# Parking weight sums whole, copying the second weights a batch later, and making the sums of u on VectorE

## The chip, the cores and the metric

The kernel runs on one core of a Trainium2 chip. The metric is the device time of one execution in microseconds. Three runs of the kernel before took 598.86, 599.93 and 600.01; the median is 599.93.

## The reference

A local attention feeds a mixer of two pairs of linear layers. All tensors are float32.

```python
# q, k, v: (4, 8, 768, 64); block, window = 32, 16
k_sum = k.reshape(B, H, nb, block, D).max(axis=3)
v_sum = v.reshape(B, H, nb, block, D).mean(axis=3)
mask_l = np.abs(pos[:, None] - pos[None, :]) < window
scores = concat([where(mask_l, scale * q @ k.T, -1e9), scale * q @ k_sum.T + log(block)])
x = softmax(scores) @ concat([v, v_sum])              # -> x: (4, 768, 512)
# mixer, w_tok1 (768, 256), w_tok2 (256, 768), w_ch1 (512, 1536), w_ch2 (1536, 512)
h = np.maximum(x.transpose(0, 2, 1) @ w_tok1, 0.0) @ w_tok2
u = x + h.transpose(0, 2, 1)
out = u + np.maximum(u @ w_ch1, 0.0) @ w_ch2
```

## The kernel before

**A planner orders the work.** Each piece of work is handed to `add(engine, took, run, reads, writes, rank, behind, kb)`. `Plan._order` then walks a model of the five queues (`pe`, `act`, `dve`, `pool`, `sp`): a work becomes ready when what it reads has been written and its tile is free, each queue takes the ready work of the lowest rank, then the earliest added, and the result is a fixed order per engine. `took` is the model's duration. A DMA costs `sp` 0.06 us of the model, and all DMAs share one line: `dma = max(dma, now) + w.kb / self.RATE` with `RATE` 250 (KB per us), and `LAND` 2.2 us on top. The ranks are `R_H, R_EVAC, R_ATT, R_LATER, R_W, R_BACK`, from 0 to 5; DMAs have rank 0. `behind` orders without waiting for the end: `state["gate"]` holds back parts of a slot's side work until that slot's first matmul has been started in the model. Tiles have tags with a number of buffers ("h" 2, "t1" 4, "u0" 4, "e" 3, "w1" and "w2" 12); the n-th tile of a tag waits until all users of the tile that many places before it are done.

**Precision.** A float32 operand is split into a high part rounded to `float32r` (an ACT copy) and a low part (the difference). Each product is then three matmuls (`HL`): high by high, high by low, low by high.

**Stages.** The four batches run one after the other, `b` = 0 to 3. In a batch of the first three the mixer's second pair of layers has 24 slots: `half` 0 (512 columns) with `f` = 0 to 11, then `half` 1 (256 columns). A slot is `ch1` (twelve matmuls to bank `hp`, line 852, then `h` split on ACT, line 864, and DVE, line 869) and `ch2` (twelve matmuls into `acc`, line 895). Beside the slots of batch `b` runs all that batch `b + 1` needs before its own: attention (`att_step`: `scores`, `turn_blocks`, `weighted`), `tok1x` and `tok2`, which give `u`. From the third batch on (`FAR`), the probabilities `e` are turned through DRAM: a DVE block transpose (line 511), one DMA to `away`, four fetches to `eT` (line 530), and then the `av` products (line 557); `x` goes the same way by `xaway` to `xT`, or to the tiles `u` (`u32`) of the last batch. `finish` adds `acc` to `u` on DVE (line 926, tile `ot` of tag "h"), adds the low part on POOL (line 934) and stores (line 945).

**The last batch** multiplies in 2 x 2 blocks with seven products instead of eight (`last_mix`). It needs sums of weight blocks (`s1` to `s4`) for both layers, and sums of `u` blocks (`t_1` to `t_4`, each split). Every product of six matmuls is ordered after the one before it. In the first phase each of six `k` has the products "11", "s2", "s3", "12", "s1" and, one `k` later by `later(k)`, "s4" and "22". Their banks are `pa`, `pb`, `pc`. `from_bank` (line 1098, DVE) adds a bank to a tile. In the second phase each of the seven names has six `k`, with banks `qa`, `qb`, `qc`; its right side is split just before use into tiles `x..` of tag "u0" (lines 1083 and 975).

**The weight sums** are made ahead by `weight_sums(w, k, tag)`, twelve calls at the slots `SUMS = ((14, 17), (6, 8, 10, 13, 15), (6, 8, 10, 12, 14))` of the three batches: five POOL and six DVE operations on 128x256 (`between`, lines 973 and 975), two ACT roundings (line 1035), two POOL differences (line 1040), and four DMAs of 256 KB to `sums` (line 1048). `weight_away(f)` copies the split second weights, 512 KB each, to `w2d` (line 1057) in slots 0 to 11 of the second batch. `first_load` fetches both parts of `s1` to `s4` for the first phase (line 1170, tags "t1" and "u1"), `second_loads` fetches the second phase's weights (line 1209, `rs` from `sums` and `r` from `w2d`) into the tiles that held the first weights.

Of the kernel before, what the change touches and what calls it, by code (L numbers as in the profile page):

```python
# [23 lines left out]
P = 128  # L24
# [165 lines left out]
def tile_attention_mixer(  # L190
# [788 lines left out]
    def weight_sums(w, k, tag):  # L979

        blk, keys = blocks(w, k)
        away = sd[w, k] = plan.slot(dram, [P, 2, 4, 256], F32, "sums", f"sums_{w}_{k}", 2 * HALF)
        gate = state["gate"]
        one = {}

        def part(name, i):
            return (lambda: blk[name](i)), keys

        def pair(n):
            if tag == "t1":  # L990
                lo, hi = (
                    sbuf([P, 2, 256], tag, f"s{x}_{w}_{k}_{n}", 4) for x in "lh"
                )
                views = [lambda: lo.t, lambda: hi.t]
                slots = (lo, "lo"), (hi, "hi")
            else:
                slot = sbuf([P, 2, 2, 256], tag, f"s_{w}_{k}_{n}", 2)
                views = [lambda: slot.t[:, 0], lambda: slot.t[:, 1]]
                slots = (slot, "lo"), (slot, "hi")
            return views, [[(s, (x, i)) for i in range(2)] for s, x in slots]  # L1000

        for n in range(2):
            (lo, hi), (lkeys, hkeys) = pair(n)
            one[n] = lo, hi, lkeys, hkeys

            def own(i, lo=lo, lkeys=lkeys):
                return (lambda: lo()[:, i]), [lkeys[i]]

            def old(i, x):
                lo0, hi0, lk0, hk0 = one[0]  # L1010
                return ((lambda: lo0()[:, i]), [lk0[i]]) if x else ((lambda: hi0()[:, i]), [hk0[i]])

            def step(eng, i, left, right, op, lo=lo, lkeys=lkeys):
                add(
                    eng, 0.78 if eng == "pool" else 0.36,
                    lambda: between(eng, lo()[:, i], left[0](), right[0](), op),
                    reads=left[1] + right[1], writes=[lkeys[i]], rank=R_BACK, behind=gate,
                )

            if n == 0:  # L1020
                step("pool", 0, part("21", 0), part("22", 0), ALU.add)
                step("pool", 0, own(0), part("21", 1), ALU.add)
                step("pool", 0, own(0), part("22", 1), ALU.add)
                step("pool", 1, own(0), part("11", 0), ALU.subtract)
                step("pool", 1, own(1), part("11", 1), ALU.subtract)
            else:
                step("dve", 0, part("11", 0), part("21", 0), ALU.subtract)
                step("dve", 0, own(0), part("11", 1), ALU.add)
                step("dve", 0, own(0), part("21", 1), ALU.subtract)
                step("dve", 1, part("12", 0), old(1, 0), ALU.subtract)  # L1030
                step("dve", 1, own(1), old(1, 1), ALU.subtract)
                step("dve", 1, own(1), part("12", 1), ALU.add)
            add(
                "act", 0.65,
                lambda lo=lo, hi=hi: nc.scalar.activation(hi().bitcast(F32R), lo(), AF.Copy),  # L1035
                reads=lkeys, writes=hkeys, rank=R_BACK,
            )
            add(
                "pool", 1.3,
                lambda lo=lo, hi=hi: nc.gpsimd.tensor_tensor(  # L1040
                    out=lo().bitcast(F32R), in0=lo(), in1=hi(), op=ALU.subtract
                ),
                reads=hkeys, writes=lkeys, rank=R_BACK,
            )
            for i, (view, vkeys) in enumerate(((hi, hkeys), (lo, lkeys))):
                add(
                    "sp", 0.06,
                    lambda i=i, n=n, view=view: nc.sync.dma_start(
                        out=away.t[:, i, 2 * n : 2 * n + 2], in_=view()
                    ),  # L1050
                    reads=vkeys, writes=[(away, (n, i))], kb=262,
                )
# [8 lines left out]

    def last_mix():

        b = B - 1
        order = []

        def pe(took, run, reads, writes):
            order.append(
                add("pe", took, run, reads=reads, writes=writes, rank=R_W, behind=order[-1:])
            )  # L1070

        def both(eng, out_, left, right, op, rank):
            (o, oi), (l, li), (r, ri) = out_, left, right
            add(
                eng, 1.05 if eng == "pool" else 0.5,
                lambda: between(eng, o.t[:, oi], l.t[:, li], r.t[:, ri], op),
                reads=[left, right], writes=[out_], rank=rank,
            )

        def split(src, view, keys, eng, rank=R_EVAC):  # L1080
            s, i = src
            add(
                "act", 0.44, lambda: nc.scalar.activation(view(0), s.t[:, i], AF.Copy),
                reads=[src], writes=keys[:1], rank=rank,
            )
            add(
                eng, 1.05 if eng == "pool" else 0.5,
                lambda: between(
                    eng, view(1), s.t[:, i], view(0).bitcast(F32), ALU.subtract
                ),  # L1090
                reads=[src, keys[0]], writes=keys[1:], rank=rank,
            )
# [28 lines left out]
        def piece(slot, pre=()):  # L1121
            def view(i):
                t = slot.t
                for k in pre:
                    t = t[:, k]
                return t[:, i]

            return view, [(slot, (*pre, i)) if pre else (slot, i) for i in range(2)]

        B11, B12, B21, B22 = u32[0, 0], u32[1, 0], u32[0, 1], u32[1, 1]  # L1130
        tmp = sbuf([P, 4, HS], "wt", "t32", 3)
        tmp3 = sbuf([P, 2, HS], "h", "t33", 2)
        x2s = sbuf([P, 2, 2, HS], "x", "t_2", 2, F32R)
        x3s = sbuf([P, 2, 2, HS], "x", "t_3", 2, F32R)
        ops = {
            "11": [piece(u_t.pop((b, 0, j))) for j in range(2)],
            "21": [piece(u_t.pop((b, 0, 2 + j))) for j in range(2)],
            "22": [piece(u_t.pop((b, 1, 2 + j))) for j in range(2)],
            "t2": [piece(x2s, (j,)) for j in range(2)],
            "t3": [piece(x3s, (j,)) for j in range(2)],  # L1140
        }
        for j in range(2):
            both("dve", (tmp, j), (B12, j), (B11, j), ALU.subtract, R_ATT)
            both("dve", (tmp, 2 + j), (B22, j), (tmp, j), ALU.subtract, R_ATT)
            split((tmp, 2 + j), *ops["t2"][j], "dve", R_ATT)
        for j in range(2):
            both("pool", (tmp3, j), (B22, j), (B12, j), ALU.subtract, R_ATT)
            split((tmp3, j), *ops["t3"][j], "pool", R_ATT)
        ops["t1"] = [piece(sbuf([P, 2, HS], "e", f"t_1_{j}", 3, F32R)) for j in range(2)]
        ops["t4"] = [  # L1150
            piece(sbuf([P, 2, HS], *(("e", "t_4_0", 3), ("h", "t_4_1", 2))[j], F32R))
            for j in range(2)
        ]
        for j in range(2):
            split((tmp, j), *ops["t1"][j], "dve", R_ATT)
            both("dve", (tmp3, j), (B21, j), (tmp, 2 + j), ALU.subtract, R_ATT)
            split((tmp3, j), *ops["t4"][j], "pool", R_ATT)


        RING = ("s2", "s4", "s3", "s1")  # L1160

        def first_load(k):
            tag = ("t1", "u1")[k % 2]
            away, got = sd[1, k], {}
            for name in RING:
                slot = got[name] = sbuf([P, 2, 2, P], tag, f"{name}_{k}", 4, F32R)
                i = int(name[1]) - 1
                add(
                    "sp", 0.06,
                    lambda slot=slot, i=i: nc.sync.dma_start(  # L1170
                        out=slot.t.bitcast(F32).rearrange("p i c f -> p i (c f)"),
                        in_=away.t[:, :, i],
                    ),
                    reads=[(away, (i // 2, j)) for j in range(2)], writes=[(slot, 0)], kb=262,
                )
            return got
# [16 lines left out]
        def second_loads():  # L1193
            for name, _, _ in SECOND:
                for m in range(HALF // 2):
                    slot = wring[name, m] = sbuf([P, 2, 2, 256], "w1", f"r{name}_{m}", NF, F32R)
                    for j in range(2):
                        k = 2 * m + j
                        if name[0] == "s":
                            away, i = sd[2, k], int(name[1]) - 1  # L1200
                            src, keys = (lambda away=away, i=i: away.t[:, :, i]), [(away, (i // 2, x)) for x in range(2)]
                        else:
# [3 lines left out]
                            keys = [(away, 0)]  # L1206
                        add(
                            "sp", 0.06,
                            lambda slot=slot, j=j, src=src: nc.sync.dma_start(
# [318 lines left out]
    for b in range(B - 1):  # L1528
# [19 lines left out]
        for slot, (half, f) in enumerate(seq):  # L1548
# [54 lines left out]
            if b == 1 and slot < NF:  # L1603
                weight_away(slot)
# [64 lines left out]
```

## Time and profile before

| | |
|---|---|
| profiled execution | 600.4 us |
| its span | 598.6 us |
| mean granted TensorE clock | 0.977 |
| TensorE matmuls busy | 567.8 us, 95% |
| VectorE (DVE) busy | 371.2 us, 62% |
| GpSimd (POOL) busy | 260.8 us, 44% |
| ScalarE (ACT) busy | 257.0 us, 43% |
| DMA | 112.12 MB, 187 GB/s on average |
| `sums` written | 48 DMAs of 256 KB |
| `sums` read | 48 DMAs of 256 KB |
| `w2d` written | 12 DMAs of 512 KB |

The span runs from the first to the last instruction; the execution's time has 1.8 us more around it. All times in the views count from the span's start. The first batch's slots end at about 207 us, the second's at about 332, the third's at about 498; from there the last batch's two phases run, the second from 550. A row of the timeline gives start, duration, engine, line, operation, tile written from tiles read, and in brackets how long the engine had stood idle before it and what ended that.

### The profile page before, as it was taken

The page shows a single profiled execution, that of the slowest core. Times are in us where ns is not written, and L with a number is a line of the kernel's source. Part 1 is how long each engine was busy: PE and PEld are TensorE (multiplying, and loading weights), DVE is VectorE, ACT ScalarE, POOL GpSimd, SP SyncE. Part 2 cuts the span into 40 slices and gives each one's busy share as a digit, 9 for nine tenths or more (in the row PEclk, how much of TensorE's full clock was granted, in tenths as well). Part 3 has the DMA queues.
Part 4 walks back from the last instruction along what each step waited for, and adds up shares of the span by engine and source line. Part 5 has one row for each costly group of instructions (what it writes and reads, how often), then busy time and mean ns, then how long its engine had stood idle before and what let it go on. Part 6 is the DMA issues. An engine that isn't in the chain of part 4 may idle for free.

```text
span 598.6 us, 12794 instructions
## 1 busy us (share of the span) xinstructions
PE 567.8 (95%) x4629; PEld 495.2 (83%) x4629; DVE 371.2 (62%) x1006; ACT 257.0 (43%) x777; POOL 260.8 (44%) x301
## 2 busy tenths in 40 slices
PE   8899999989999999999999769999999997999997
PEld 4688878768889978877999647777789986999997
DVE  4688799986874353586354445457564862335875
ACT  4667575445674242333244224343343332334542
POOL 0225586745365210344646700034449834344611
PEclk8889999999999999999999988999999998999999
DMA  8943568644755157888839754677675533578731
GB/s 268 324 148 121 181 199 261 220 146 160 244 177 193 60 187 224 225 294 262 258 100 277 168 113 134 140 182 203 190 190 147 140 124 124 187 230 270 245 105 73
DMA packets 143375, 112.12 MB, mean 187 GB/s; under 512 B 88656, under 2 KB 118992, under 8 KB 143312
## 3 DMA queue, kind: packets, MB, share of 16 engines
q1 hardware_dynamic: 143168, 111.10, 62.3%
q8 instruction: 37, 0.61, 0.4%
q14 instruction: 26, 0.21, 0.1%
q10 hardware_dynamic: 144, 0.20, 0.1%
HBM read 74.90 MB, written 34.60 MB: 183 GB/s over the span
## 4 chain that ended last, share of the span: by engine, by line
PE 64%; DVE 11%; DMA 8%; POOL 6%; issue 3%; SPq 3%; ACT 3%; DVEq 0%; POOLq 0%; ACTq 0%
PE acc L895 17%; PE hp L852 17%; PE sc L426 3%; PE av L557 3%; PE pb L1115 3%; PE qb L1115 3%; DMA w<-in_w_ch 3%; PE qa L1115 2%; PE t1q L747 2%; PE pc L1115 2%; PE pa L1115 2%; PE qc L1115 2%; PE up L791 2%; POOL ot L934 2%; DVE wb L1451 1%
## 5 line engine op out<-in xcount | busy, mean ns | idle before, releaser
L852 PE MATMUL hp<-u,w 128*128 128x512 f32 (+1 forms) x864 | 166.7, 342 | 2.8 <-DVE u L975 1.5
L895 PE MATMUL acc<-h,w 128*128 128x512 f32 (+1 forms) x864 | 165.9, 341 | 3.2 <-DVE h L869 2.2
L852 PEld LDWEIGHTS hp<-u,w 128*128 128x128 f32 x864 | 134.4, 190 | 25.0 <-DVE u L975 2.6
L895 PEld LDWEIGHTS acc<-h,w 128*128 128x128 f32 x864 | 133.4, 189 | 24.8 <-DVE h L869 3.2
L450 ACT ACTIVATE e<-e,den 128x120 f32<-128x120 f32 x192 | 73.3, 384 | 48.1 <-DVE den L440 48.0
L869 DVE SCALAR_TENSOR_TENSOR h<-hp,h 128x512 fp32r<-128x512 f32 (+1 forms) x72 | 39.7, 551 | 68.0 <-ACT h L864 67.7
L864 ACT ACTIVATE h<-hp 128x512 fp32r<-128x512 f32 (+1 forms) x72 | 35.0, 487 | 94.6 <-PE hp L852 94.6
L440 DVE CUSTOM_DVE_ANT_0 e<-sc,mask_sb 128x120 f32<-128x120 f32 x192 | 41.5, 276 | 9.5 <-PE sc L426 5.5
L1480 POOL TENSOR_TENSOR w<-wb,w 128x256 fp32r<-128x256 f32 x48 | 37.9, 810 | 17.8 <-ACT w L1474 17.5
L791 PE MATMUL up<-wt,t 128*128 128x512 f32 (+2 forms) x192 | 40.4, 353 | 1.9 <-DVE t L686 1.4
L934 POOL TENSOR_TENSOR ot<-ot,u 128x512 f32<-128x512 f32 (+1 forms) x24 | 23.8, 1020 | 29.0 <-DVE ot L926 29.0
L450 ACT ACTIVATION_READ_ACCUMULATOR e<-e,den 128x1 f32 x192 | 36.2, 188 | 0.0
L791 PEld LDWEIGHTS up<-wt,t 128*128 128x128 f32 x192 | 31.1, 192 | 5.4 <-DVE t L686 1.9
L1040 POOL TENSOR_TENSOR sl<-sl,sh 128x512 fp32r<-128x512 f32 x12 | 15.5, 1289 | 44.0 <-ACT sh L1035 44.0
L747 PE MATMUL t1q<-xs,ws 128*128 128x256 f32 x216 | 29.4, 285 | 4.0 <-POOL ws L733 3.4
L747 PEld LDWEIGHTS t1q<-xs,ws 128*128 128x128 f32 x216 | 27.2, 190 | 5.4 <-POOL ws L733 4.2
L557 PEld LDWEIGHTS av<-v,eT 120*64 120x64 f32 x768 | 24.0, 138 | 8.0 <-issue 5.6
L557 PE MATMUL av<-v,eT 120*64 120x64 f32 x768 | 26.6, 224 | 4.2 <-DMA eT<-away 2.2
L426 PE MATMUL sc<-k,q 64*64 64x120 f32 x768 | 28.4, 275 | 1.8 <-PE et L488 0.7
L426 PEld LDWEIGHTS sc<-k,q 64*64 64x64 f32 x768 | 20.9, 135 | 10.4 <-issue 5.9
L570 DVE TENSOR_TENSOR x<-av,rec 128x384 f32<-128x384 f32 x32 | 17.4, 552 | 18.7 <-PE av L557 17.6
L1474 ACT ACTIVATE w<-wb 128x256 fp32r<-128x256 f32 x48 | 18.1, 413 | 23.8 <-DVE wb L1451 23.7
(141 smaller groups left out, 919.6 us busy)
## 6 DMA issues: line engine op xcount, KB each, us to landing
w<-in_w_ch SPq DMA_DIRECT2D x48, 256.0 KB
k<-in_kw SPq DMA_DIRECT2D x16, 720.0 KB
v<-in_vw SPq DMA_DIRECT2D x32, 288.0 KB
q<-in_q SPq DMA_DIRECT2D x16, 384.0 KB
sums<-s SPq DMA_DIRECT2D x24, 256.0 KB
w2d<-w SPq DMA_DIRECT2D x12, 512.0 KB
away<-e SPq DMA_DIRECT2D x16, 384.0 KB
eT<-away SPq DMA_DIRECT2D x64, 96.0 KB
```

Of the source, the lines that this page charges most:

```text
L426: nc.tensor.matmul(tiles[j].t[c * QT : (c + 1) * QT, i * NC : (i + 1) * NC], lhsT=qt.t[rows, t * QT : (t + 1) * QT], rhs=kt.t[rows, t, :], ...
L440: nc.vector.tensor_tensor_reduce(out=e.t[:, j, i * P : i * P + NC], in0=tiles[j].t[:, i * NC : (i + 1) * NC], in1=mask_sb[:, mv, :], op0=A ...
L450: nc.scalar.activation(ei, ei, AF.Exp, bias=den_t[n].t[:, 1, T : T + 1], scale=-1.0, accum_out=den_t[n].t[:, 0, T : T + 1],)
L557: nc.tensor.matmul(pv[cs, T], lhsT=eT[:NC, T % (TT // 2), cs], rhs=v.t[:NC, 2 * T + c], start=True, stop=True,)
L747: nc.tensor.matmul(pt.t[:, 2 * P * k : 2 * P * (k + 1)], lhsT=ws[:, wp, T, ks], rhs=xs[:, xp, T], start=(c == 0 and k == 0 and T == 0 and ...
L791: nc.tensor.matmul(pt.t[:, :nt], lhsT=t1.t[:, part, ks], rhs=wt2[w].t[:, k, h0 : h0 + nt], start=(far and k == 0 and i == 0), stop=(k == D ...
L852: nc.tensor.matmul(pt.t[:, :nt], lhsT=w1_t[f].t[:, w, c], rhs=us[c].t[:, part], start=(i == 0), stop=(i == len(ops) - 1),)
L869: lambda: nc.vector.scalar_tensor_tensor(out=h.t[:, 1], in0=pt.t[:, :nt], scalar=0.0, in1=h.t[:, 0].bitcast(F32), op0=ALU.max, op1=ALU.sub ...
L895: nc.tensor.matmul(slot.t[:, c0 : c0 + nt], lhsT=w2_t[f].t[:, w, o * P : (o + 1) * P], rhs=h.t[:, part], start=(f == 0 and w == 0 and part ...
L934: lambda view=view, u=u: nc.gpsimd.tensor_tensor(out=view(), in0=view(), in1=u.t[:, 1].bitcast(F32), op=ALU.add),
L1115: nc.tensor.matmul(bank_.t[:, :HS], lhsT=w(i), rhs=x(j), start=first and n == 0, stop=True, skip_group_check=True,)
L1480: lambda hi=hi, lo=lo, source=source: nc.gpsimd.tensor_tensor(out=lo(), in0=source(), in1=hi().bitcast(F32), op=ALU.subtract),
```

## The change

Five things are changed.

1. `weight_sums` parks each sum as whole float32. The ACT rounding and POOL difference are gone, each pair of sums is one DMA of 256 KB instead of two, and `s4` is made from the whole `s2` in two DVE operations instead of three. In the slots with tag "h" one tile holds all four sums where there were two tiles; with tag "t1" two tiles instead of four.
2. `parted` splits a parked sum after it has been fetched: in the first phase an ACT copy and a DVE difference on 256 columns for each of 24 fetches (rank `R_EVAC`), in the second phase on 512 columns for each of 12 tiles (rank `R_LATER`). The fetches of sums are 128 KB each instead of 256.
3. `weight_away` is called in slots 12 to 23 of the third batch instead of slots 0 to 11 of the second.
4. The sums of `u` move from the start of `last_mix` to `last_sums`, called in slot 22 of the third batch, ahead of that batch's `finish`. The difference for `t_3` and the low parts of `t_3` and `t_4`, six operations, go from POOL to DVE. The helpers `both`, `split` and `piece` are moved out of `last_mix` unchanged.
5. The second phase's product "11" for `k` 0 and 1 is ordered ahead of `later(5)`, the end of the first phase.

```diff
     def weight_sums(w, k, tag):
...
-        away = sd[w, k] = plan.slot(dram, [P, 2, 4, 256], F32, "sums", f"sums_{w}_{k}", 2 * HALF)
+        away = sd[w, k] = plan.slot(dram, [P, 4, 256], F32, "sums", f"sums_{w}_{k}", 2 * HALF)
...
+        if tag == "t1":
+            z = [sbuf([P, 2, 256], tag, f"s_{w}_{k}_{n}", 4) for n in range(2)]
+            at = [(z[i // 2], i % 2) for i in range(4)]
+        else:
+            z = sbuf([P, 4, 256], tag, f"s_{w}_{k}", 2)
+            at = [(z, i) for i in range(4)]
...
+        step("pool", 0, part("21", 0), part("22", 0), ALU.add)
+        step("pool", 0, own(0), part("21", 1), ALU.add)
+        step("pool", 0, own(0), part("22", 1), ALU.add)
+        step("dve", 2, part("11", 0), part("21", 0), ALU.subtract)
+        step("dve", 2, own(2), part("11", 1), ALU.add)
+        step("dve", 2, own(2), part("21", 1), ALU.subtract)
+        step("pool", 1, own(0), part("11", 0), ALU.subtract)
+        step("pool", 1, own(1), part("11", 1), ALU.subtract)
+        step("dve", 3, part("12", 0), own(1), ALU.subtract)
+        step("dve", 3, own(3), part("12", 1), ALU.add)
         for n in range(2):
...
-            add(
-                "act", 0.65,
-                lambda lo=lo, hi=hi: nc.scalar.activation(hi().bitcast(F32R), lo(), AF.Copy),
...
-            add(
-                "pool", 1.3,
-                lambda lo=lo, hi=hi: nc.gpsimd.tensor_tensor(
-                    out=lo().bitcast(F32R), in0=lo(), in1=hi(), op=ALU.subtract
...
+                lambda n=n, view=view: nc.sync.dma_start(
+                    out=away.t[:, 2 * n : 2 * n + 2], in_=view()
                 ),
...
+    def last_sums():
...
         for j in range(2):
-            both("pool", (tmp3, j), (B22, j), (B12, j), ALU.subtract, R_ATT)
-            split((tmp3, j), *ops["t3"][j], "pool", R_ATT)
+            both("dve", (tmp3, j), (B22, j), (B12, j), ALU.subtract, R_ATT)
+            split((tmp3, j), *ops["t3"][j], "dve", R_ATT)
...
             split((tmp, j), *ops["t1"][j], "dve", R_ATT)
             both("dve", (tmp3, j), (B21, j), (tmp, 2 + j), ALU.subtract, R_ATT)
-            split((tmp3, j), *ops["t4"][j], "pool", R_ATT)
+            split((tmp3, j), *ops["t4"][j], "dve", R_ATT)
...
+        def parted(slot, hi, lo, cols):
+            rank = R_EVAC if cols == 256 else R_LATER
+            add(
+                "act", 0.42 if cols == 256 else 0.65,
+                lambda: nc.scalar.activation(hi(), lo().bitcast(F32), AF.Copy),
+                reads=[(slot, "raw")], writes=[(slot, "hi")], rank=rank,
+            )
+            add(
+                "dve", 0.38 if cols == 256 else 0.62,
+                lambda: between(
+                    "dve", lo(), lo().bitcast(F32), hi().bitcast(F32), ALU.subtract
+                ),
+                reads=[(slot, "hi")], writes=[(slot, "raw"), (slot, 0), (slot, 1)], rank=rank,
+            )
...
             if k + 2 < HALF:
                 rings[k + 2] = first_load(k + 2)
-        later(HALF - 1)
...
+        for k in range(2):
+            second(*SECOND[0], k)
+        later(HALF - 1)
         for name, rhs, to in SECOND:
+            for k in range(2 * (name == "11"), HALF):
+                second(name, rhs, to, k)
...
-            if b == 1 and slot < NF:
-                weight_away(slot)
+            if b == B - 2 and slot >= NF:
+                weight_away(slot - NF)
+            if b == B - 2 and slot == 22:
+                last_sums()
```

More of the change, by code (lines that the diff above doesn't have):

```diff
@@ L986, in part @@
         def part(name, i):
             return (lambda: blk[name](i)), keys
[L989 to L1000, printed above, removed]
@@ L1002, in weight_sums @@
-        for n in range(2):
[L1003 to L1013, printed above, removed]
-                add(
[L1015 to L1032, printed above, removed]
-            add(
-                "act", 0.65,
-                lambda lo=lo, hi=hi: nc.scalar.activation(hi().bitcast(F32R), lo(), AF.Copy),
-                reads=lkeys, writes=hkeys, rank=R_BACK,
-            )
-            add(
-                "pool", 1.3,
-                lambda lo=lo, hi=hi: nc.gpsimd.tensor_tensor(
-                    out=lo().bitcast(F32R), in0=lo(), in1=hi(), op=ALU.subtract
[L1042 to L1052, printed above, removed]
@@ new lines, in own, with step @@
+        def own(i):
+            slot, j = at[i]
+            return (lambda: slot.t[:, j]), [at[i]]
+        def step(eng, i, left, right, op):
+            add(
+                eng, 0.78 if eng == "pool" else 0.38,
+                lambda: between(eng, own(i)[0](), left[0](), right[0](), op),
+                reads=left[1] + right[1], writes=[at[i]], rank=R_BACK, behind=gate,
+            )
+        step("pool", 0, part("21", 0), part("22", 0), ALU.add)
+        step("pool", 0, own(0), part("21", 1), ALU.add)
@@ L1060, in weight_away, with both, split @@
         )
+    def both(eng, out_, left, right, op, rank):
+        (o, oi), (l, li), (r, ri) = out_, left, right
+        add(
+            eng, 1.05 if eng == "pool" else 0.5,
+            lambda: between(eng, o.t[:, oi], l.t[:, li], r.t[:, ri], op),
+            reads=[left, right], writes=[out_], rank=rank,
+        )
+    def split(src, view, keys, eng, rank=R_EVAC):
+        s, i = src
+        add(
+            "act", 0.44, lambda: nc.scalar.activation(view(0), s.t[:, i], AF.Copy),
+            reads=[src], writes=keys[:1], rank=rank,
+        )
+        add(
+            eng, 1.05 if eng == "pool" else 0.5,
+            lambda: between(
+                eng, view(1), s.t[:, i], view(0).bitcast(F32), ALU.subtract
+            ),
+            reads=[src, keys[0]], writes=keys[1:], rank=rank,
+        )
@@ new lines, in piece, with view @@
+    def piece(slot, pre=()):
+        def view(i):
+            t = slot.t
+            for k in pre:
+                t = t[:, k]
+            return t[:, i]
+        return view, [(slot, (*pre, i)) if pre else (slot, i) for i in range(2)]
+    ops = {}
+    def last_sums():
+        b = B - 1
+        B11, B12, B21, B22 = u32[0, 0], u32[1, 0], u32[0, 1], u32[1, 1]
+        tmp = sbuf([P, 4, HS], "wt", "t32", 3)
+        tmp3 = sbuf([P, 2, HS], "h", "t33", 2)
+        x2s = sbuf([P, 2, 2, HS], "x", "t_2", 2, F32R)
+        x3s = sbuf([P, 2, 2, HS], "x", "t_3", 2, F32R)
+        ops.update({
+            "11": [piece(u_t.pop((b, 0, j))) for j in range(2)],
+            "21": [piece(u_t.pop((b, 0, 2 + j))) for j in range(2)],
+            "22": [piece(u_t.pop((b, 1, 2 + j))) for j in range(2)],
+            "t2": [piece(x2s, (j,)) for j in range(2)],
+            "t3": [piece(x3s, (j,)) for j in range(2)],
+        })
+        for j in range(2):
+            both("dve", (tmp, j), (B12, j), (B11, j), ALU.subtract, R_ATT)
+            both("dve", (tmp, 2 + j), (B22, j), (tmp, j), ALU.subtract, R_ATT)
+            split((tmp, 2 + j), *ops["t2"][j], "dve", R_ATT)
+        for j in range(2):
+            both("dve", (tmp3, j), (B22, j), (B12, j), ALU.subtract, R_ATT)
+            split((tmp3, j), *ops["t3"][j], "dve", R_ATT)
+        ops["t1"] = [piece(sbuf([P, 2, HS], "e", f"t_1_{j}", 3, F32R)) for j in range(2)]
+        ops["t4"] = [
+            piece(sbuf([P, 2, HS], *(("e", "t_4_0", 3), ("h", "t_4_1", 2))[j], F32R))
+            for j in range(2)
+        ]
+        for j in range(2):
+            split((tmp, j), *ops["t1"][j], "dve", R_ATT)
+            both("dve", (tmp3, j), (B21, j), (tmp, 2 + j), ALU.subtract, R_ATT)
+            split((tmp3, j), *ops["t4"][j], "dve", R_ATT)
@@ L1062, in last_mix @@
     def last_mix():
         b = B - 1
+        B11, B12, B21, B22 = u32[0, 0], u32[1, 0], u32[0, 1], u32[1, 1]
         order = []
@@ L1069, in pe @@
                 add("pe", took, run, reads=reads, writes=writes, rank=R_W, behind=order[-1:])
[L1070 to L1091, printed above, removed]
             )
@@ L1119, in products @@
                     n += 1
[L1121 to L1145, printed above, removed]
@@ L1170, in first_load @@
                     lambda slot=slot, i=i: nc.sync.dma_start(
-                        out=slot.t.bitcast(F32).rearrange("p i c f -> p i (c f)"),
-                        in_=away.t[:, :, i],
+                        out=slot.t[:, 1].bitcast(F32).rearrange("p c f -> p (c f)"),
+                        in_=away.t[:, i],
                     ),
-                    reads=[(away, (i // 2, j)) for j in range(2)], writes=[(slot, 0)], kb=262,
+                    reads=[(away, i // 2)], writes=[(slot, "raw")], kb=131,
                 )
+                parted(slot, lambda slot=slot: slot.t[:, 0], lambda slot=slot: slot.t[:, 1], 256)
             return got
@@ L1200, in second_loads @@
                             away, i = sd[2, k], int(name[1]) - 1
-                            src, keys = (lambda away=away, i=i: away.t[:, :, i]), [(away, (i // 2, x)) for x in range(2)]
+                            src = lambda away=away, i=i: away.t[:, i]
+                            to = lambda slot=slot, j=j: slot.t[:, j, 1]
+                            reads, key, kb = [(away, i // 2)], "raw", 131
                         else:
@@ new lines, in second, with run @@
+        def second(name, rhs, to, k):
+            src = {
+                "h11": lambda: (hA[k], 0), "h21": lambda: (hB[k], 0), "h22": lambda: (hB[k], 1),
+                "t3": lambda: (hA[k], 1), "t1": lambda: (tt[k // 2], k % 2),
+                "t2": lambda: (tt[k // 2], 2 + k % 2), "t4": lambda: (tt[k // 2], 2 + k % 2),
+            }[rhs]()
+            if rhs == "t4":
+                both("pool", src, (hB[k], 0), src, ALU.subtract, R_LATER)
+            view, keys = piece(sbuf([P, 2, HS], "u0", f"x{name}_{k}", 4, F32R))
+            split(src, view, keys, "dve")
+            ring = wring[name, k // 2]
+            for r in range(2):
+                bank_ = banks[to][r]
+                def run(bank_=bank_, r=r, start=k == 0 and to not in seen):
+                    w = lambda i: ring.t[:, k % 2, i, r * P : (r + 1) * P]
+                    products(bank_, [w], [view], start)
+                pe(0.53, run, keys + [(ring, k % 2)], [(bank_, 0)])
```

57 lines of the change are left out of this document (19 added, 38 removed).

## The prediction

> **What bounds the kernel now.** I read the engine shares first, then the busy time by stretches, the chain that ended last, and the timeline of the two stretches where TensorE stands still. TensorE is busy 95% of the span, so only its pauses and its slow-clock time can be won.
>
> ```profile
> PE 567.8 (95%) x4629; PEld 495.2 (83%) x4629; DVE 371.2 (62%) x1006; ACT 257.0 (43%) x777; POOL 260.8 (44%) x301
> 300.00:330.00 30.00, 30.00 (x307) 29.51 (x306) 16.22 (x57) 11.57 (x40) 15.74 (x19) 1.00 0.63 185
> 330.00:360.00 30.00, 21.03 (x159) 15.75 (x157) 12.89 (x27) 7.74 (x14) 12.12 (x14) 0.94 0.63 139
> 360.00:370.00 10.00, 10.00 (x67) 7.88 (x60) 5.94 (x31) 5.72 (x27) 0.00 (x0) 0.83 0.34 93
> 460.00:470.00 10.00, 9.02 (x68) 8.82 (x67) 6.74 (x9) 5.21 (x11) 9.75 (x8) 1.00 0.55 122
> 480.00:490.00 10.00, 8.58 (x70) 8.18 (x70) 7.76 (x17) 5.18 (x11) 3.58 (x3) 1.00 0.40 132
> 490.00:500.00 10.00, 10.00 (x81) 9.88 (x79) 2.69 (x7) 1.68 (x4) 3.30 (x5) 1.00 0.12 41
> 500.00:510.00 10.00, 6.00 (x19) 5.08 (x18) 2.46 (x3) 1.95 (x4) 5.41 (x6) 0.67 0.54 173
> 540.00:550.00 10.00, 9.35 (x53) 9.03 (x53) 6.00 (x12) 4.83 (x11) 3.00 (x3) 1.00 0.99 316
> ```
>
> Columns: stretch, length, busy time of PE, PEld, DVE, ACT, POOL, then granted clock, DMA share, GB/s. Of 30.8 us without TensorE work, 9.0 lie in 330-360 (second batch hands over to third), 4.0 in 500-510 (third hands over to last), 0.65 in 540-550 (between the last batch's two phases). After both hand-overs the clock falls too: 0.83 costs 1.7 us of 360-370.
>
> **Hand-over to the last batch (term 1).** `t_3` and `t_4` are made on POOL late:
>
> ```profile
> 491.92 1.01 POOL L973 TENSOR_TENSOR t<-u,u 128x384 f32<-128x384 f32 x1 [2.49 <-DMA sums<-s]
> 497.71 2.82 POOL L934 TENSOR_TENSOR ot<-ot,u 128x256 f32<-128x256 f32 x4 [4.78 <-DVE ot L926]
> 499.86 0.34 PE L1115 MATMUL pc<-t,s 128*128 128x384 f32 x1
> 505.50 1.01 PE L1115 MATMUL pc<-t,s 128*128 128x384 f32 x2 [0.94 <-POOL t L973]
> 506.51 1.92 PE pa L1115 x6
> 525.10 1.06 PE pa L1115 x6
> 507.59 0.52 ACT L1083 ACTIVATE t<-t 128x384 fp32r<-128x384 f32 x1 [3.77 <-DMA out<-ot]
> 486.47 0.54 DVE L975 SCALAR_TENSOR_TENSOR t<-t,t 128x384 fp32r<-128x384 f32 x1
> ```
>
> The first difference starts at 491.92, when a parked sum has left the "h" tile that it takes; its low part then queues behind the four adds of `finish`. So the product pc, six matmuls worth 1.06, holds TensorE from 499.86 to 506.51: 5.6 us lost, and the next two products cost 1.92 instead of 1.06 each (1.7 us): 7.3 in all. The change makes `t_3` and `t_4` on DVE, adds them at slot 22, and orders their "h" tiles ahead of `finish`'s, with one tile per parked sum instead of two. DVE takes over six operations at 0.54 (3.2 us) that stood on POOL; it is busy 7.76 of 480-490 but 2.69 of 490-500, so they fit before 497. `t_4_1` no longer waits for stores (the 3.77); instead `finish`'s tile waits for the last reading of `t33`, with DVE's queue behind it. That is late only if `t_4` is, and the last `t_2` split stands at 486.47, ten us earlier. I take -6.5; ends -7.3 and -2 (if `t_4`, needed two products after `s1`, becomes the next late one).
>
> **Hand-over from second to third batch (term 2).** Attention for the next batch turns its probabilities through DRAM; its `av` products mark its pace. First the chain's rows, then two timeline rows:
>
> ```profile
> 239.76 1.55 PE av L557 x48
> 270.47 1.55 PE av L557 x48
> 309.20 1.55 PE av L557 x48
> 382.07 1.55 PE av L557 x48
> ...
> 405.38 1.27 PE av L557 x36
> 431.17 1.57 PE av L557 x48
> 333.53 1.27 PE L557 MATMUL av<-v,eT 120*64 120x64 f32 x36 [1.33 <-DMA eT<-away]
> 456.34 1.62 PE L557 MATMUL av<-v,eT 120*64 120x64 f32 x48
> L1057 SPq DMA_DIRECT2D w2d<-w x12: 428/554/2619, 202.1 to 282.5; - x12
> 202.00:283.00 81.00, 81.00 (x607) 65.05 (x606) 46.72 (x146) 26.40 (x95) 20.67 (x28) 1.00 0.74 224
> ```
>
> Four `av` pairs take 239.8 to 333.5, 94 us, in the second batch, and 382.1 to 456.3, 74 us, in the third, which has no `w2d` copies. The last `av` of the second batch comes after all its `ch2` work, and everything behind it (t1, the `xT` fetches, u) is bare. The planner prices transfers in one line at 250 KB per us: twelve copies of 524 are 25 us of it, and halved parking (2 x 262 fewer per block) takes 2.1 us off each of the five blocks. The stretch that holds the copies moved 224 x 81 = 18.1 MB, 73 us at the planner's rate out of 81. Without copies and half the sums of the first three blocks it is some 41. So the plan need not hold `eT` back. At the third batch's pace the last `av` comes 19 us earlier, and about 10 are enough to cover the pause. Apart from that:
>
> ```profile
> 335.83 1.30 POOL L1040 TENSOR_TENSOR s<-s 128x512 fp32r<-128x512 f32 x1
> 337.08 1.31 POOL L733 TENSOR_TENSOR xs<-x,xs 128x512 fp32r<-128x512 f32 x1
> 341.39 0.57 SPq L1048 DMA_DIRECT2D sums<-s  x1
> 347.73 6.67 SPq L530 DMA_DIRECT2D xT<-xaway  x10
> ```
>
> The low part at 335.83 stands before the first `xs` (1.2 us), and a parked half sits in SP's unbroken run of fetches (0.6): both vanish, which is the least, -2. The most is -10.7 (9.0 idle and 1.7 clock). I take -8, nearer the pace seen in the third batch.
>
> **Gap between phases (term 3).** The first two `k` of product "11" (four groups of three 384-column matmuls, about 2.1 us by the 1.06 row) now stand before `later(5)`, which waited on DVE:
>
> ```profile
> PE pb L1115 <- DVE hb L1098: 0.7, 1, 0.7
> ```
>
> -0.6; ends -0.65 and 0.
>
> **Parked sums, first half (term 4).** Per block two ACT and two POOL operations (1.30 each on POOL), two SP issues (0.57) and one DVE operation (0.41) go, twelve times. Outside 330-360 TensorE mostly covers them: 0, ends -2.4 (the pauses of 460-470, 1.0, and 480-490, 1.4) and 0.
>
> **The copies in the third batch (term 5).** Twelve issues at about 0.55 (6.6 us of SP) and 6.3 MB now come between the slots of 440-497, among `eT` and `u` fetches; at the 316 GB/s of 540-550 they are 20 us of a stretch whose DMA share sinks to 0.40 and 0.12 at its end. SP's queue holds the `u` fetches behind them. Ten us of slack before `t_3` is needed hide that; +0.5, ends 0 and +9 (rival below).
>
> **Splitting at use (term 6).** First the kinds of operation, then three stretches of the second phase:
>
> ```profile
> L1474 ACT ACTIVATE w<-wb 128x256 fp32r<-128x256 f32 x48 | 18.1, 413 | 23.8 <-DVE wb L1451 23.7
> L975 DVE SCALAR_TENSOR_TENSOR sl<-w,sh 128x256 f32<-128x256 f32 x6 | 2.5, 410 | 0.0
> L975 DVE SCALAR_TENSOR_TENSOR u<-xT,u 128x512 fp32r<-128x512 f32 x4 | 2.8, 690 | 0.9 <-ACT u L818 0.7
> L975 DVE SCALAR_TENSOR_TENSOR xs<-ha,xs 128x384 fp32r<-128x384 f32 x2 | 2.7, 1368 | 0.0
> L975 DVE SCALAR_TENSOR_TENSOR xs<-hb,xs 128x384 fp32r<-128x384 f32 x6 | 3.3, 553 | 1.0 <-ACT xs L1083 1.0
> 552.00:558.00 6.00, 6.00 (x36) 6.00 (x35) 4.70 (x6) 3.76 (x8) 4.54 (x5) 1.00 0.79 242
> 558.00:564.00 6.00, 6.00 (x36) 6.00 (x35) 5.83 (x7) 2.85 (x6) 5.04 (x5) 1.00 0.81 253
> 564.00:570.00 6.00, 6.00 (x36) 6.00 (x35) 4.95 (x9) 3.16 (x6) 2.34 (x2) 1.00 0.76 244
> ```
>
> First phase: 24 ACT and 24 DVE operations on 256 columns at 0.41 (first two rows), four each per `k` (seven products of 1.06, 7.4 us): 1.6 us each per `k`, beside DVE at 6.0 and ACT at 4.8 of the ten us of 540-550. I take 0; the end is +1.5, where ACT waits for a ring's DMA with bank evacuations queued behind it. Second phase: 12 each on 512 columns, 0.69 on DVE (third row). DVE is busy 15.5 of the 18 us of 552-570 (splits take 1.37 beside POOL's `t_4` work and 0.55 without it). About seven of the twelve low parts (rings of s2's end, s3, s1) belong there: 4.8 us, 2.3 too many, against splits that run up to four tiles ahead. +1.0; ends 0 and +5.7.
>
> **Sum.** 600.4 (profiled execution: span 598.6 and 1.8 around it) - 6.5 - 8 - 0.6 + 0 + 0.5 + 1.0 = 586.8; the median of the runs is 0.5 lower than the profiled execution, so 586.3.
>
> **Rivals.**
> A shared path of DVE and POOL: by the 1.37 row each low part costs 1.37 while POOL works. Seven are 9.6 us; with 15.5 that is 7.1 over 18, less three tiles of lead (3.2): 3.9 us of waiting, and one more slow-clock stretch like the 1.7: +5.7 instead of +1.0, so 591. Against it: POOL is idle in 570-576, and the parts may slip there. The Trainium skill (SBUF — State Buffer, "Who interferes with whom") says that a DVE instruction with two SBUF inputs and a GpSimd instruction that reads SBUF block each other whole, which speaks against putting work on DVE here; the rows agree (1.37 against 0.55).
>
> Only the last hand-over is mended: if attention's tile turns, not the copies, set its pace, term 2 stays at its end: 592.3. For it: the third batch too takes 25 us per `av` pair without copies. Against it: the second needs 31 and 39 between its first three.
>
> Only the other is mended: `t_4` or a ring is late next, term 1 stays at its end: 590.8.
>
> Slower: the moved copies hold the `u` fetches. They add 25 us to the planner's line in the third batch and parking's saving takes 4 off, 21 net. If the `u` tiles come 21 later, the last `t_2` split moves from 487 to 508 against 498.6 where it is used: 9.4 us of waiting and 1.7 of clock, 11.1 instead of 7.3. With term 2 at -2, term 3 and the second phase as above: 600.4 + 3.8 - 2 - 0.6 + 1.0 = 602.6, so 602. It decides from a delay of some 12 us on. Against it: the line is empty late, with a DMA share of 0.12 in 490-500.
>
> The pauses bring their own slow clock: the rows show 0.67 only where TensorE waited 4.0 us in ten. By the Trainium skill (TensorE: Matmul & The Clock Gate, "What's actually happening") about 3.4 us of idling halve the clock; the trace agrees, and the 1.7 us parts go only if the pauses do.
>
> **How the numbers follow.** Both hand-overs mended as summed: 0.45. Only the last: 0.22; only the other: 0.13; DVE and POOL in each other's way: 0.10; copies too late: 0.10. The range runs from all gains at their ends (600.4 - 7.3 - 10.7 - 0.65 - 2.4 - 0.5 = 578.9) to 598, which takes in the mended cases with the second phase or the copies at their dear ends and leaves out the slower case. Within 0.2% (1.2 us, about what runs of this kernel can tell) needs gains and losses to cancel: 0.04; slower 0.10; faster 0.86.
>
> **What would show it.** Term 1: no POOL releaser on pc, clock 1.00 in the ten us after the third batch. Term 2: the last `av` of the second batch stands before its last `ch2`, and that hand-over has under 3 us without TensorE work. Term 3: no wait of pb on DVE hb. Term 5: the `u` fetches end no more than 5 us later against the end of the third batch. Term 6: TensorE unbroken in the second phase, DVE near full. The prediction fails if attention in the second batch keeps its pace, if `u` is late in the third, or if a newly ordered queue opens a pause elsewhere.

## The result, and the profile after

The changed kernel takes 580.69 us (four runs, 579.63 to 584.92) against 599.97 before: a ratio of 0.9689 with a 95% interval of 0.9634 to 0.9744. The forecast was 586.3 in 579 to 598. The profiled execution took 584.92, the longest of the four, with a span of 582.4.

First the page of the changed kernel and the stretches of the two hand-overs (columns as above):

```profile
PE 562.4 (97%) x4629; PEld 491.2 (84%) x4629; DVE 389.2 (67%) x1036; ACT 257.4 (44%) x789; POOL 226.0 (39%) x271
300.00:330.00 30.00, 29.79 (x272) 28.71 (x271) 19.08 (x32) 10.33 (x22) 25.74 (x25) 1.00 0.70 190
330.00:360.00 30.00, 30.00 (x232) 26.38 (x231) 13.47 (x46) 9.26 (x34) 3.84 (x7) 1.00 0.32 86
480.00:490.00 10.00, 10.00 (x74) 10.00 (x73) 3.31 (x8) 1.81 (x5) 2.82 (x4) 1.00 0.23 73
490.00:500.00 10.00, 10.00 (x59) 10.00 (x58) 7.58 (x15) 5.74 (x16) 3.19 (x3) 1.00 0.64 204
```

Both hand-overs (about 346 and 485 now) run without a pause and at full clock. To see each stage by itself, I cut both traces at the same products: the second batch's first `ch1`, the third batch's first `ch2`, the first `pa` of the last batch, the first `qb`, and the end of the matmuls. Between them lies the same TensorE work (the counts differ by one record). Before, then after:

```profile
209.60:365.40 155.80, 146.83 (x1163) 122.76 (x1161) 83.45 (x252) 51.88 (x168) 58.70 (x68) 0.98 0.71 202
365.40:497.70 132.30, 129.00 (x1036) 112.51 (x1033) 78.61 (x210) 47.41 (x147) 60.27 (x64) 1.00 0.62 164
497.70:556.40 58.70, 54.05 (x291) 52.69 (x290) 25.33 (x44) 20.84 (x43) 27.18 (x29) 0.94 0.68 217
556.40:594.90 38.50, 38.50 (x217) 37.58 (x216) 28.77 (x45) 17.91 (x35) 13.83 (x11) 1.00 0.42 138
```

```profile
212.20:353.90 141.70, 141.49 (x1162) 120.31 (x1160) 81.56 (x246) 45.77 (x157) 46.90 (x58) 1.00 0.60 163
353.90:485.20 131.30, 129.69 (x1037) 112.53 (x1034) 77.11 (x218) 45.08 (x145) 45.53 (x53) 1.00 0.68 189
485.20:535.70 50.50, 50.50 (x291) 50.50 (x290) 38.68 (x64) 28.19 (x64) 23.20 (x23) 1.00 0.48 149
535.70:578.70 43.00, 39.78 (x217) 36.91 (x215) 36.18 (x55) 21.76 (x43) 15.17 (x12) 1.00 0.33 110
```

| stage | before | after | difference |
|---|---|---|---|
| start to the second batch's first `ch1` | 209.6 | 212.2 | +2.6 |
| second batch, to the third's first `ch2` | 155.8 | 141.7 | -14.1 |
| third batch, to the first `pa` | 132.3 | 131.3 | -1.0 |
| hand-over and first phase, to the first `qb` | 58.7 | 50.5 | -8.2 |
| rest of the second phase | 38.5 | 43.0 | +4.5 |

The first row holds a pause of 2.2 us ahead of an `av` product at 162 us (1.0 before; more on it at the end of the experiments). It also varies by itself: with the old rate of the planner's line it runs from 205.4 to 212.2 us in the kept traces, and the kernel before and the run with unpriced copies, whose edit first acts at about 200 us, have 209.6 and 205.4. So totals that lie a few us apart say less than the later stages. The other four rows make -18.8, which is nearly the whole difference of the medians, -19.3.

The second batch's attention now keeps its pace. Timeline rows of TensorE, with that batch's last `ch2` at the end:

```profile
236.69 1.62 PE L557 MATMUL av<-v,eT 120*64 120x64 f32 x48
261.80 1.62 PE L557 MATMUL av<-v,eT 120*64 120x64 f32 x48
287.88 1.62 PE L557 MATMUL av<-v,eT 120*64 120x64 f32 x48
313.10 1.62 PE L557 MATMUL av<-v,eT 120*64 120x64 f32 x48
343.61 3.02 PE L895 MATMUL acc<-h,w 128*128 128x256 f32 x24
```

Four pairs take 76 us (94 before), and the last comes 30 us before the last `ch2`, not after it. At the other hand-over the six products of pc follow without a break, since DVE has made all the `t` tiles by 477.0, 7.7 us before `finish`:

```profile
475.98 1.01 DVE L975 SCALAR_TENSOR_TENSOR t<-t,t 128x384 fp32r<-128x384 f32 x2
484.65 1.48 DVE L926 TENSOR_TENSOR ot<-acc,u 128x256 f32<-128x256 f32 x4 [1.30 <-PE acc L895]
487.30 1.20 PE L1131 MATMUL pc<-t,s 128*128 128x384 f32 x6
488.34 1.20 PE L1131 MATMUL pa<-u,w 128*128 128x384 f32 x6
```

The loss is in the second phase. Four stretches, then TensorE's two waits there:

```profile
528.00:534.00 6.00, 6.00 (x36) 6.00 (x35) 5.27 (x9) 3.71 (x8) 2.39 (x3) 1.00 0.56 181
534.00:540.00 6.00, 5.43 (x30) 4.81 (x28) 6.00 (x6) 5.20 (x12) 5.51 (x5) 1.00 0.85 267
540.00:546.00 6.00, 4.04 (x21) 3.37 (x21) 6.00 (x7) 3.03 (x6) 4.21 (x4) 1.00 0.12 39
546.00:552.00 6.00, 5.36 (x29) 4.66 (x28) 6.00 (x11) 2.92 (x6) 2.29 (x2) 1.00 0.54 173
PE qb L1131 <- DVE xs L975: 2.0, 3, 0.8
PE qc L1131 <- DVE xs L975: 1.2, 2, 0.6
```

DVE has no idle time from 534 to 552, yet gets through only six and seven operations in the first two of these stretches, while POOL works. TensorE does 21 matmuls in 540-546, where an unbroken stretch has 36, and waits 3.2 us for DVE's splits in all.

### The profile page after: what moved, and what is told of

Read it like the earlier page. It is cut to its first block, busy times and chain, and to the rows that moved or that the text cites. A ratio compares the mean times of both kernels' runs of the same rounds, so it can differ in the third digit from the quotient of the medians.

```text
span 582.4 us, 12756 instructions
## 1 busy us (share of the span) xinstructions
PE 562.4 (97%) x4629; PEld 491.2 (84%) x4629; DVE 389.2 (67%) x1036; ACT 257.4 (44%) x789; POOL 226.0 (39%) x271
## 4 chain that ended last, share of the span: by engine, by line
PE 69%; DVE 12%; DMA 8%; issue 3%; POOL 3%; ACT 2%; SPq 1%; DVEq 0%; ACTq 0%; POOLq 0%
PE acc L895 19%; PE hp L852 18%; PE av L557 4%; PE t1q L747 4%; PE sc L426 3%; DMA w<-in_w_ch 3%; PE pb L1131 3%; PE up L791 3%; PE qa L1131 2%; DMA away<-e 2%; PE pc L1131 2%; PE pa L1131 2%; PE qb L1131 2%; PE qc L1131 2%; DVE wb L1453 2%
## 5 line engine op out<-in xcount | busy, mean ns | idle before, releaser
L852 PE MATMUL hp<-u,w 128*128 128x512 f32 (+1 forms) x864 | 163.7, 339 | 0.0
L852 PEld LDWEIGHTS hp<-u,w 128*128 128x128 f32 x864 | 133.0, 188 | 20.5 <-issue 1.3
L409 POOL MEMSET e<- 128x48 f32 x16 | 2.2, 138 | 107.6 <-DMA away<-e 42.6
L791 PE MATMUL up<-wt,t 128*128 128x512 f32 (+2 forms) x192 | 39.2, 345 | 0.4 <-DVE u L808 0.3
L973 POOL TENSOR_TENSOR s<-s,w 128x256 f32<-128x256 f32 x48 | 36.8, 768 | 3.4
L733 POOL TENSOR_TENSOR xs<-x,xs 128x512 fp32r<-128x512 f32 x18 | 24.2, 1343 | 19.3 <-ACT xs L728 19.3
L426 PEld LDWEIGHTS sc<-k,q 64*64 64x64 f32 x768 | 21.3, 136 | 10.7 <-issue 6.6
```

Of the source, the lines that this page charges most:

```text
L426: nc.tensor.matmul(tiles[j].t[c * QT : (c + 1) * QT, i * NC : (i + 1) * NC], lhsT=qt.t[rows, t * QT : (t + 1) * QT], rhs=kt.t[rows, t, :], ...
L791: nc.tensor.matmul(pt.t[:, :nt], lhsT=t1.t[:, part, ks], rhs=wt2[w].t[:, k, h0 : h0 + nt], start=(far and k == 0 and i == 0), stop=(k == D ...
L852: nc.tensor.matmul(pt.t[:, :nt], lhsT=w1_t[f].t[:, w, c], rhs=us[c].t[:, part], start=(i == 0), stop=(i == len(ops) - 1),)
L973: nc.gpsimd.tensor_tensor(out=out_, in0=left, in1=right, op=op)
```

## Experiments

**Is it the copies' place?** My theory: the copies in the second batch made its attention late. The rival: the halved parking traffic and the POOL and ACT work that went with it. First the copies alone put back into the changed kernel:

```diff
-            if b == B - 2 and slot >= NF:
-                weight_away(slot - NF)
+            if b == 1 and slot < NF:
+                weight_away(slot)
```

> The changed kernel with the twelve copies of the second weights back in slots 0 to 11 of the second batch, all else as changed. If the copies' place is what freed attention in the second batch (155.9 us before, 141.7 after, from the first ch1 to the second ch2 slot of the next batch), this run loses 9 to 14 us against the changed kernel: 590 to 595, the last av pair again after about 320, and a hand-over pause of 5 us or more. If instead the halved parking traffic and the POOL and ACT operations that went with it did it, the copies do no harm: 580 to 584.

Measured: 589.72 us, ratio 0.9814 (0.9754 to 0.9874), just under the range; the second batch's stage is 152.5, with its last `av` pair at 328.18. Then the same place as the only change of the kernel before (the inverse edit):

> The kernel before with nothing changed but the copies' place (slots 12 to 23 of the third batch). If the place is the cause in the second batch, 9 to 14 us go there: 586 to 591 in all, with both parts of the sums still parked and the last hand-over unmended or a few us worse. If the parking traffic is the cause, 597 to 600.

Measured: 580.54, ratio 0.9677 (0.9636 to 0.9718), below the range that I gave. The second batch's stage, with the copies put back into the changed kernel and then with the copies moved in the kernel before:

```profile
208.50:361.00 152.50, 146.24 (x1162) 123.15 (x1160) 83.92 (x246) 45.80 (x158) 46.25 (x58) 0.97 0.68 190
209.50:350.80 141.30, 141.30 (x1163) 120.25 (x1161) 85.45 (x251) 51.21 (x167) 58.73 (x68) 1.00 0.67 182
```

The third batch, which has the copies in the second of these runs, takes 131.1 there. Both say the place: with the copies elsewhere nothing else is needed in this stage, and with them there the rest of the change brings 3.3 us (155.8 to 152.5). The surprise is the total: these two lines alone reach what the whole change reaches. So all the other edits add up to nearly nothing. The stages show why: -8.2 and +4.5 in the last batch, of which this run has 1.2 too (57.5 for 58.7), and 0.6 back in the second and third. That leaves 1.8 us (368.3 here from the second batch's first `ch1` to the end of the matmuls, 366.5 in the changed kernel), which the longer first batch of the changed kernel hides (212.2 and 209.5).

**Traffic or price?** The copies load the DMA engines and SP, but they also take 25 us in the planner's line of transfers, by which it orders the work. Two runs separate these. In the kernel before, the same copies at the same place, but priced at next to nothing:

```diff
-            reads=[(w2_t[f], 0), (w2_t[f], 1)], writes=[(away, 0)], kb=524,
+            reads=[(w2_t[f], 0), (w2_t[f], 1)], writes=[(away, 0)], kb=1,
```

> The kernel before with the copies in their old place in the second batch, but priced at 1 KB instead of 524 in the planner's line of transfers. The real DMAs and bytes stay. If the planner's price made attention in the second batch late (it ordered work as if 25 us of line were taken), that batch's stage falls from 155.8 to 142-147 and the time to 586-591. If the real transfers and SP's issues held attention up, it stays at 152-156: 597-601.

And the copies moved, with only their price left behind:

```diff
+            if b == 1 and slot < NF:
+                add("sp", 0.06, lambda: None, kb=524, behind=state["gate"])
```

> The kernel before with the copies in slots 12 to 23 of the third batch (141.3 us for the second batch's stage, 580.5 in all), and with twelve empty works of 524 KB in the planner's line in slots 0 to 11 of the second batch: no DMA is issued there. If the price alone orders attention late, the stage rises to 150-156 and the time to 590-596; if only real traffic counts, it stays at 141-143 and 580-582.

Measured: 588.26 (ratio 0.9807, 0.9762 to 0.9852) and 594.09 (0.9892, 0.9857 to 0.9926). The second batch's stage, real copies without price, then price without copies:

```profile
205.40:347.80 142.40, 141.76 (x1163) 120.64 (x1161) 84.96 (x251) 51.04 (x167) 59.95 (x68) 1.00 0.77 221
205.50:362.40 156.90, 146.83 (x1163) 122.75 (x1161) 82.78 (x252) 51.84 (x168) 58.43 (x68) 0.98 0.60 164
```

The stage with the highest DMA share of all, 0.77, is quick, and the one with no copy in it, 0.60, is as slow as before. The last four `eT` fetches are issued 118.6 us after the start of the stage in the second one, 100.2 in the first, and the last `av` pair of the second one again waits for its tiles:

```profile
305.03 1.62 PE L557 MATMUL av<-v,eT 120*64 120x64 f32 x48
327.52 0.57 PE L557 MATMUL av<-v,eT 120*64 120x64 f32 x12
329.59 1.27 PE L557 MATMUL av<-v,eT 120*64 120x64 f32 x36 [1.50 <-DMA eT<-away]
```

That settles it: the copies' bytes cost the stage some 1 us at most (142.4, and 141.3 with the copies elsewhere). Their price made the rest, through the order that the planner wrote.

**Is the price then simply too high?** In the version with `t_4` on DVE (below) I raised the rate of the whole line:

```diff
-    RATE, LAND = 250.0, 2.2
+    RATE, LAND = 320.0, 2.2
```

> The changed kernel with t_4 on DVE (577.1), and the planner's line of transfers at 320 KB per us instead of 250, near the 316 GB/s of the busiest stretch before. If the price still orders work too late anywhere, the third batch's stage of 130.6 falls by 1 to 3 us: 573 to 576. If nothing waits on the price any more, 576 to 579; if the plan now counts on transfers that land later, new waits on DMA appear: over 580.

Measured: 596.25 (ratio 0.9922, 0.9886 to 0.9958), 19 us worse than that version. The longest waits of TensorE (`vm` and `t1p` belong to attention's means of `v` and to `tok1x`):

```profile
PE av L557 <- DMA eT<-away: 7.9, 4, 2.8
PE vm L338 <- DMA v<-in_vw: 5.4, 4, 3.2
PE t1p L700 <- DVE wt L1453: 2.7, 1, 2.7
```

The plan now puts products ahead of transfers that have not landed, and TensorE, which keeps to the plan's order, stands (17.5 us idle before the second batch, 12.0 in that version). The second and third batch take 149.1 and 135.7 us, where that version has 141.7 and 130.6. So the old price is a useful one for most transfers, as far as this one other rate tells; it was wrong for copies on which nothing waits until the last batch.

**The hand-over to the last batch: engine, place or tiles?** Four runs, each the changed kernel with a part of it undone. The sums of `u` back on POOL and back behind `finish`:

```diff
-            if b == B - 2 and slot == 22:
-                last_sums()
+    last_sums()
     last_mix()
...
-            both("dve", (tmp3, j), (B22, j), (B12, j), ALU.subtract, R_ATT)
-            split((tmp3, j), *ops["t3"][j], "dve", R_ATT)
+            both("pool", (tmp3, j), (B22, j), (B12, j), ALU.subtract, R_ATT)
+            split((tmp3, j), *ops["t3"][j], "pool", R_ATT)
...
-            split((tmp3, j), *ops["t4"][j], "dve", R_ATT)
+            split((tmp3, j), *ops["t4"][j], "pool", R_ATT)
```

> The changed kernel with the sums of u back at the start of the last stage and their six operations back on POOL, all else as changed. If the late POOL chain made the hand-over to the last batch, it costs 6 to 7.5 us again: 587 to 588, with pc waiting on POOL t and a slow clock behind it. If the hand-over was mended by the smaller ring loads and the single tile per parked sum, which stay, it costs under 2: 581 to 583.

Measured: 588.56 (ratio 0.9796, 0.9747 to 0.9846), stage 57.9 instead of 50.5, with the old rows back:

```profile
487.67 1.01 POOL L973 TENSOR_TENSOR t<-u,u 128x384 f32<-128x384 f32 x1
487.77 0.62 PE L1131 MATMUL pc<-t,s 128*128 128x384 f32 x2 [1.33 <-POOL t L973]
491.92 1.01 PE L1131 MATMUL pc<-t,s 128*128 128x384 f32 x2 [1.12 <-POOL t L973]
```

Only the engine undone (the second half of that diff):

> The changed kernel with the sums of u still in slot 22 of the third batch, but their six operations on POOL as before. If the place (ahead of finish, early tiles of tag h) mends the hand-over, the stage to s2 stays at 50.5 to 51.5 and the time at 580 to 582; if the engine does, pc or the product of t_4 waits for POOL again, the stage is 54 to 58 and the time 584 to 588.

Measured: 583.58 (ratio 0.9718, 0.9687 to 0.9748), stage 50.5; the third batch takes 1.5 more. Only the place undone (the first half):

> The changed kernel with the sums of u on DVE, but back at the start of the last stage, behind finish. With POOL and late, the stage from the last batch's first product to s2 was 57.9; with POOL in slot 22 it was 50.5. If only the place and the order of the h tiles count, it stays bad: t_4_1 waits for the stores of finish's tile, 53 to 57 us, and 583 to 588 in all. If DVE alone would also do, 50.5 to 52 and 580 to 582.

Measured: 581.80 (ratio 0.9684, 0.9642 to 0.9725), stage 52.2. I had expected it bad. So, with the sums parked whole, either will do: by the stages early on POOL costs 1.5 us, late on DVE 1.7, and only late on POOL costs 7.4. Then the parking back in two parts, everything else as changed (`weight_sums`, `first_load` and `second_loads` of the kernel before, no `parted`):

> The changed kernel with the sums parked split into two parts as before (no splitting at use), the copies, the sums of u and the order of product 11 as changed. The second phase should go back from 43.0 to 38.5 us. If the hand-over to the last batch is mended by DVE and the place of the sums of u alone, the stage from the last batch's first product to the second phase's s2 stays at 50.5: 573 to 576 in all, under the changed kernel by 5 to 7. If it needs the single tile per parked sum (two tiles of tag h make t33 late), the stage is 53 to 58 and the time 577 to 582.

Measured: 580.71 (ratio 0.9662, 0.9609 to 0.9715), level with the changed kernel. The second phase is short again (39.1), but the hand-over stage is 57.7 although the sums of `u` are on DVE and early. Twelve products of the third batch lie in it, 1.4 us, since this plan runs the first `pa` before them (302 records for 291; one product left none); so the loss is 5.8, not 7.2. The two stages, waits of TensorE, DVE and SP rows, and a piece of the chain that ended last:

```profile
476.10:533.80 57.70, 54.29 (x302) 53.33 (x301) 26.49 (x51) 20.85 (x45) 21.59 (x23) 0.97 0.71 223
533.80:572.90 39.10, 39.09 (x217) 37.30 (x216) 30.57 (x45) 17.90 (x35) 14.67 (x12) 1.00 0.42 136
PE pc L1160 <- DMA s<-sums: 2.3, 1, 2.3
PE pb L1160 <- DMA s<-sums: 0.9, 1, 0.9
479.47 0.56 DVE L975 SCALAR_TENSOR_TENSOR t<-t,t 128x384 fp32r<-128x384 f32 x1 [0.23 <-ACT t L1073]
480.14 1.42 DVE L926 TENSOR_TENSOR ot<-acc,u 128x256 f32<-128x256 f32 x4
485.78 0.52 SPq L1176 DMA_DIRECT2D s<-sums  x1
485.78 5.25 DMA s<-sums
```

The `t` tiles are done only at 480, `finish` follows at once behind them in DVE's order, the "u1" tiles come free late, and the second ring (the four 256 KB loads of `s1` to `s4` for the second `k`, into the "u1" tiles), issued up to 485.78, lands when pc is already waiting (491.07). That is close to the new wait that I had named as possible, `finish` behind the last reading of `t33`; whether its tile or only DVE's order holds `finish`, the rows do not tell. Nor does a run separate the two tiles per parked sum from the larger loads. So parking whole gains 5.8 us here and gives 4.0 back in the second phase.

**The second phase: count or shared path?**

```diff
                 if rhs == "t4":
-                    both("pool", src, (hB[k], 0), src, ALU.subtract, R_LATER)
+                    both("dve", src, (hB[k], 0), src, ALU.subtract, R_LATER)
```

> The changed kernel with the six differences for t_4 in the second phase on DVE instead of POOL. In the changed kernel that phase takes 4.5 us more than before and DVE is busy without a break from 534 to 552, its operations taking 1.37 to 1.5 us beside POOL ones and 0.55 to 0.68 without. If the shared path is the cause, taking POOL away wins 3 to 4.5 us though DVE has six operations more: 576 to 578. If DVE simply has too many operations, six more cost 2 to 4: 582 to 585.

Measured: 577.08 (574.95 to 577.93), ratio 0.9604 (0.956 to 0.9648), the best kernel here. The rest of the second phase takes 39.3. Groups of DVE in the changed kernel from 528 to 556, then in this one at the same place, 524 to 552:

```profile
L975 DVE SCALAR_TENSOR_TENSOR xs<-th,xs 128x384 fp32r<-128x384 f32 x12 | 10.4, 884 | 0.3 <-ACT xs L1044 0.3
L975 DVE SCALAR_TENSOR_TENSOR rs<-rs 128x512 fp32r<-128x512 f32 x10 | 8.8, 884 | 0.1
```

```profile
L975 DVE SCALAR_TENSOR_TENSOR xs<-th,xs 128x384 fp32r<-128x384 f32 x12 | 7.9, 674 | 0.0
L975 DVE SCALAR_TENSOR_TENSOR rs<-rs 128x512 fp32r<-128x512 f32 x10 | 7.2, 716 | 0.1
L975 DVE SCALAR_TENSOR_TENSOR th<-hb,th 128x384 f32<-128x384 f32 x6 | 3.2, 542 | 0.0
```

The two groups shrink from 19.2 to 15.1 us, which pays for the six operations that DVE took over (3.2), and TensorE waits 0.2 us for DVE there instead of 3.2. It is not the path alone: without `parted` POOL's `t_4` does no harm (39.1 in the run above). Both together overfill DVE.

**Again, the changed kernel.**

> The changed kernel once more, beside the two runs below on one chip: 579 to 583, with stages 141.7, 131.2, 50.5 and 43.0 us. The pause of 2.2 us before an av product in the first batch, which no step of the change explains, should be another size or gone if it belongs to the one execution.

Measured: 581.67 (579.21 to 584.17), ratio 0.9685 (0.963 to 0.9741), stages 141.6, 130.6, 50.5, 43.3. The pause in the first batch did not go:

```profile
PE av L557 <- issue: 2.7, 1, 2.7
```

It is 1.0 us long in the kernel before, 0.6 and 0.3 in the runs with unpriced copies and with parking in two parts. Over the kept traces at the old rate it is 1.8 to 2.7 us in the six with whole parking and moved copies and 0.3 to 1.2 in the other six, so it seems to go with the change and not with one execution. What makes it I have not tried; it stays open.

## Why the prediction was right, and where not

The time lies in the range, and both hand-overs were mended, as the likeliest case had it. The sum was 5.6 us too high (586.3 against 580.7): term 2 won 6.1 us more than summed, terms 1, 3 and 5 another 2.6, and term 6 gave 3.5 back. That the time stayed above the lower end of 579 is luck: with the second phase's loss taken away (577.1, `t_4` on DVE) the same change falls below it. Nor does the total speak for the terms, since two lines of the change reach it alone.

- Term 2 (second to third batch): the mechanism was right to the point, the planner's line, and the two price runs show it alone. The size was not: -14.1 against -8, beyond my end of -10.7. The failing step was to size the pause from idle time and the 0.83 of one stretch. TensorE idles 8.8 us less, but its 1,162 matmuls are also 5.3 us less "busy" (146.83 to 141.49). About 3.5 of these are slow clock: 1.7 for the 0.83 that I counted and 1.8 for the 0.94 of 330-360, which stood in the row that I showed and was left out. What makes the other 1.8 I have not traced; waits between single matmuls of a row that counts as busy would do it. The stage's length against that of equal work was the right measure. The least that I named, -2 without the copies' place, was -3.3. The signs held: the last `av` pair stands before the last `ch2`, and 0.2 us of the stage are without TensorE work.
- Term 1 and term 3 (hand-over and gap between phases): -7.1 summed, -8.2 measured. In the three runs made from the kernel before, with its order of product "11", pb's wait of 0.7 for `hb` stands; in the changed kernel it is gone. The step "DVE takes over" was not needed, the place alone does nearly as well; and the one tile per parked sum, which I named only in passing, belongs to a condition, the whole parking: with two parts the same hand-over loses 5.8.
- Term 4: nothing, as summed, in the second and third batch (273.0 us together, 272.1 with parking in two parts). Term 5: +0.5 was -1.0; the twelve copies cost the third batch nothing (131.3 and 130.6 with them in the changed kernel, 130.9 without), and the `u` fetches end no later against its end (29 us ahead of it, 27 before).
- Term 6: +4.5 against +1.0, and the sign "TensorE unbroken" failed. The failing step priced each low part at 0.69 and trusted the lead of four tiles. Beside POOL the parts and the splits averaged 0.88. The rival of the shared path (+5.7; its parts, 3.9 and 1.7, make 5.6) was the better arithmetic: 3.2 us of waits came for its 3.9, while its 1.7 of slow clock did not (granted clock 1.00). I had put it at 0.10, apart from the case with both hand-overs mended; it came together with that. The rule of the Trainium skill (SBUF — State Buffer, "Who interferes with whom") that a DVE instruction with two SBUF inputs and a GpSimd instruction that reads SBUF block each other agrees with the 1.37 us rows here and the 0.55 without POOL.
- The slower rival fell: the price of 25 us of line in the third batch moved its length by no more than 0.4 us (131.3 and 130.6 with the copies, 130.9 without).

## What to carry to other kernels

When an order is written by a model, ask of each late piece of work whether the hardware or the model's price made it late; a run with the price alone, and one with the traffic alone, tell. Price a transfer on which nothing waits apart from those on the path, and don't cheapen them all. Size a pause from the length of a stage with equal work, not from idle time, and before giving DVE more two-input work look at what POOL does in the same stretch. When a forecast comes out right, compare it term by term: here two errors partly cancelled.

## What was not expected of the hardware

The load of the DMA engines did not bound the second batch: at a share of 0.77 and 221 GB/s the stage took 142.4 us, at 0.60 and 163 GB/s 141.7. DVE and POOL side by side cost more than either's count: 22 operations of DVE went from 0.69 to 0.88 us on average (674 and 716 ns in the two groups, then 884 in both) when POOL ran six differences beside them, and the stage was 3.7 us longer (43.0 and 39.3).
